# Weights requested one matrix at a time, behind a tile's value steps: attention and a mixture of experts in one kernel

## The chip, the cores and the metric

The kernel runs on one core of a Trainium2 chip. A core has a tensor engine for matmuls (PE, with its weight loads shown as PEld), a vector engine (DVE), a scalar engine (ACT), GpSimd (POOL) and a sync engine (SP). The five run their own instruction streams and meet through semaphores. In this kernel SP and POOL issue nearly all DMA transfers. The metric is the device time of one execution in microseconds (us); lower is better.

## The reference

Two stages follow each other. The first is attention of 16 query heads over one shared key and value head, for 8 batches of 384 positions and a head size of 64. Its output is laid out as 3072 tokens of 1024 numbers. The second stage sends each token to one of 16 experts, chosen in two steps (one of 4 groups, then one of 4 experts of the group), and scales the expert's output by the product of the two softmax weights:

```python
scores = scale * np.matmul(q, k.transpose(0, 1, 3, 2))
attn = np.exp(scores - np.max(scores, axis=-1, keepdims=True))
attn = attn / (np.sum(attn, axis=-1, keepdims=True) + 1e-09)
x = (attn @ v).transpose(0, 2, 1, 3).reshape(B * S, H * D)      # 3072 x 1024
...
g_idx = np.argmax(x @ w_group, axis=1)                           # one of 4 groups
e_idx = np.argmax(xg @ w_expert[g], axis=1)                      # one of its 4 experts
h = np.maximum(xg[mask_e] @ w1[g, e], 0.0)
out[tok_idx] = (g_w * e_w)[:, None] * (h @ w2[g, e])
```

## The kernel before

**Tiles and slots.** A batch is 3 tiles of 128 positions, and a tile is 4 slots of two units; a unit is the scores of two heads for one tile. So there are 24 tiles (`NT`) and 96 slots (`NSL`), 12 to a batch (`SB`). `s0 = 12 * b` is the first slot of batch b, and `p = i % 4` is the place of slot i in its tile. One Python loop over the slots writes out the order of all instructions; nothing reorders them later.

**One slot**, in order: the scores of two units on PE (L161); the maximum on DVE (L169) and the exponential on ACT (L172); then the slot's middle. In slots 0 and 1 of a tile the middle holds queries being transposed on PE (L147) and pieces of an expert's work (`advance`). In slots 2 and 3 it holds half each of the values of the tile before (`pv`, L209: 96 matmul records per half, small ones, 32 rows deep). Then come the transposes of probabilities by DVE (L193), the normalization by POOL (`norm`, L187), and, after slot 3, `pv_out`: ACT copies the values to `xt` (L222) and POOL casts them to bf16 into `xb` (L223). Last in the slot stands what was put down for it under the key `"g"`, which is mostly DMA issues.

**What is put down for which slot.** `at(slot, where, fn, ...)` makes the entry and `run(slot, where)` carries it out. For batch b, the router's logits of its first tile come from slot `s0 + 8` on (L230, L247). The 128 tokens of that tile elect the batch's main expert: `gate_pick` at `s0 + 10` leaves its number in `idx`. `load_main(b, 0)` reads the number into a register of POOL and issues the expert's first matrix; `load_main(b, 1)` issues the second. A matrix is two DMAs on POOL's queue (`load_w`, L394), each 2 MB of fp32 in memory that becomes 1 MB of bf16 in SBUF. SP's queue takes in the same part of the batch the saved `xb` (`keep_xb`, L410), the keys and values of the next batch (L111, L112, L120) and queries (L105), in the order written, and the stores of the expert's output `y` (L476), each as soon as ACT has scaled it.

**Experts.** `main_expert(b)` begins at slot `12 * (b + 1) + 5`. It is a generator: it gives out 42 pieces, and `advance(n)` takes 3n of them, so that PE works on batch b's expert while it does the attention of batch b + 1. A group of three pieces is 8 matmuls and the eviction of their result: 8 groups with the first matrix (L419), then 6 groups with the second (L433). Each of the two matrices has two buffers.

**The end.** After the last slot come, written out by hand, the values of the last tile (`pv(NT - 1, 0, NB)`, both halves at once), the six groups left of batch 6's expert, the expert of batch 7, and a second expert for batch 7 (`second_expert`), whose number `gate_pick_second` finds at `s0 + 13`. Its two matrices are issued by `load_second(0)` and `load_second(1)`. Then a loop runs over (batch, expert) pairs that are not covered by then. In the profile below it has no turn to make.

Of the kernel before, what the change touches and what calls it, by code (L numbers as in the profile page):

```python
# [19 lines left out]
def kernel(  # L20
# [12 lines left out]
    B, H, S, D = q.shape  # L33
# [7 lines left out]
    FO = F // P  # L41
# [149 lines left out]
    def transp(u):  # L191

        nc.vector.transpose(  # L193
            out=ring[:, (u // 4) % 3, u % 4].rearrange("p h s -> p (h s)"),
            in_=st.pop(("pr", u))[:].rearrange("p h s -> p (h s)"),
        )

    def pv(t, n0, n1):

        v_sb = st["v", t // ST]  # L200
        a, z = sorted(((2 * t) % 3, (2 * t + 1) % 3))
        if n0 == 0:
            st["o", t] = [xbank() for _ in range(P // 32)]
        o = st["o", t]
        for n in range(n0, n1):
            for i in range(P // 32):
                r = slice(32 * i, 32 * (i + 1))
                for h in range(2):
                    nc.tensor.matmul(  # L209
                        out=o[i][h * D:(h + 1) * D, 0:2 * P].rearrange("d (g c q) -> d g c q", g=2, c=4),  # L210
                        lhsT=v_sb[r, n, :], rhs=ring[r, a:z + 1:z - a, :, h, ts(n, 32)],
                        start=(n == 0), stop=(n == NB - 1), tile_position=(32 * i, h * D),
                    )

    def pv_out(t):
        b, j = t // ST, t % ST
        xt = pool.tile([P, KO, P], FP32, tag="xt", name="xt", bufs=1)
        st["xt", b, j] = xt
        if j == 0:
            st["xb", b] = pool.tile([P, KO, S], BF16, tag="xb", name="xb", bufs=2)  # L220
        for i, o in enumerate(st.pop(("o", t))):
            nc.scalar.copy(out=xt[:, :, ts(i, 32)], in_=o[:, 0:2 * P].rearrange("p (c q) -> p c q", c=KO))  # L222
        nc.gpsimd.tensor_copy(out=st["xb", b][:, :, ts(j, P)], in_=xt[:])  # L223
# [167 lines left out]
    def load_w(e, n):  # L391
        w = wpool.tile([P, KO, F], BF16, tag=f"w{n + 1}", name="w")
        for o in range(0, KO, 4):
            nc.gpsimd.dma_start(  # L394
                out=w[:, o:o + 4, :], in_=(w1f, w2f)[n][ds(e, 1), :, o:o + 4, :].rearrange("o p c f -> (o p) c f")
            )
        return w

    def load_main(b, n):
        if n == 0:  # L400
            st["e", b] = nc.gpsimd.value_load(st.pop(("idx", b))[0:1, 0:1], min_val=0, max_val=GE - 1)
        st.setdefault(("w", b), []).append(load_w(st["e", b], n))

    def load_second(n):
        if n == 0:
            st["e2"] = nc.gpsimd.value_load(st.pop("idx2")[0:1, 0:1], min_val=0, max_val=GE - 1)
        st.setdefault("w_second", []).append(load_w(st["e2"], n))
# [4 lines left out]
    def expert(xb, w1, w2, result, psum, on_act=None):  # L412

        on_act = on_act or (lambda k: k % 2 == 0)
        h_t = pool.tile([P, FO, S], BF16, tag="hT", bufs=1)
        for fc in range(FO):
            hp = psum()
            for ko in range(KO):
                nc.tensor.matmul(  # L419
                    out=hp[:, 0:S], lhsT=w1[:, ko, ts(fc, P)], rhs=xb[:, ko, :], start=(ko == 0), stop=(ko == KO - 1)  # L420
                )
                if ko % (KO // 2) == KO // 2 - 1:
                    yield
            if on_act(fc):
                nc.scalar.activation(out=h_t[:, fc, :], in_=hp[:, 0:S], func=ACTF.Relu)  # L425
            else:
                nc.vector.tensor_scalar(out=h_t[:, fc, :], in0=hp[:, 0:S], scalar1=0.0, scalar2=None, op0=ALU.max)
            yield
        for j in range(ST):
            for nh in range(2):  # L430
                yp = psum()
                for fo in range(FO):
                    nc.tensor.matmul(  # L433
                        out=yp, lhsT=h_t[:, fo, ts(j, P)], rhs=w2[:, fo, ts(nh, 512)],
                        start=(fo == 0), stop=(fo == FO - 1),
                    )
                    if fo % (FO // 2) == FO // 2 - 1:
                        yield
                result(j, nh, yp, on_act(FO + 2 * j + nh))
                yield  # L440

    def scaled(gcol, store):

        ys = {}

        def result(j, nh, yp, by_act):
            if nh == 0:
                ys[j] = pool.tile([P, Dm], FP32, tag="y", name="y", bufs=3)
            y, g = ys[j], gcol()[:, j:j + 1]
            if by_act:  # L450
                nc.scalar.activation(out=y[:, ts(nh, 512)], in_=yp, func=ACTF.Copy, scale=g)
            else:
                nc.vector.tensor_scalar(out=y[:, ts(nh, 512)], in0=yp, scalar1=g, scalar2=None, op0=ALU.mult)
            if nh == 1:
                store(j, y)

        return result
# [13 lines left out]
    def main_expert(b, on_act):  # L471
        w1, w2 = st.pop(("w", b))

        def store(j, y):
            if b < B - 1:
                nc.sync.dma_start(out=out_v[b, :, j, :], in_=y[:])  # L476
            else:
                st["y", j] = y

        yield from expert(st["xb", b], w1, w2, scaled(lambda: st["gsel", b][0], store), any_bank, on_act)  # L480
# [22 lines left out]
    pending = []  # L503

    def advance(groups):
        for _ in range(3 * groups):
            while pending:
                try:
                    next(pending[0])
                    break  # L510
                except StopIteration:
                    pending.pop(0)
# [3 lines left out]
    def at(slot, where, fn, *args):  # L516
        later.setdefault((slot, where), []).append((fn, args))

    def run(slot, where):
        for fn, args in later.pop((slot, where), []):  # L520
            fn(*args)
# [4 lines left out]
    for b in range(B):  # L526
        s0 = SB * b
        for j in range(ST):
            x = s0 + 4 * j + 8
            at(x, "m2", logits, b, j)  # L530
            at(x, "w", logits_out, b, j)
            at(x + 1, "m0", logits2, b, j)
            at(x + 1, "v", logits2_out, b, j)
        for x, j0, j1 in ((s0 + 9, 0, 1), (s0 + 17, 1, ST)):
            at(x, "v", lambda b=b, j0=j0, j1=j1: st.__setitem__(("gm", b), gate_masks(b, j0, j1)))
            at(x, "v", lambda b=b: [next(st["gm", b]) for _ in range(3)])
        if b == 0:
            at(s0 + 10, "s", gate_choose, b)
            at(s0 + 10, "b", gate_score, b)
        else:  # L540
            at(s0 + 9, "m2", gate_choose, b)
            at(s0 + 9, "w", gate_score, b)
        at(s0 + 10, "w", gate_pick, b)
        at(s0 + 10, "g", load_main, b, 0)
        at(s0 + (11 if b == B - 1 else 10), "g", load_main, b, 1)
        at(s0 + 16, "g", keep_xb, b)
        at(s0 + 20, "m0", gate_count, b)
        at(s0 + 20, "v", gate_counted, b)
        x = s0 + (20 if b == B - 2 else 23)
        at(x, "w", lambda b=b: st.__setitem__(("gv", b), gate_values(b)))  # L550
        at(x, "w", lambda b=b: [next(st["gv", b]) for _ in range(3)])
        if b == B - 1:
            at(s0 + 13, "w", gate_pick_second, b)
            at(s0 + 13, "g", load_second, 0)
        if b + 1 < B:
            at(s0 + 4, "g", load_k, b + 1)
            at(s0 + 4, "g", load_v, b + 1)
            at(s0 + 8, "m0", prep_batch, b + 1)
            at(s0 + 8, "v", prep_out, b + 1)
# [72 lines left out]
    b = B - 1  # L632
    i = NSL
# [5 lines left out]
    run(i, "w")  # L639
    transp(2 * i - 2)  # L640
    transp(2 * i - 1)
    advance(1)
    run(i + 1, "m0")
    run(i + 1, "v")
    run(i + 1, "w")
    run(i + 1, "g")
    pv(NT - 1, 0, NB)
    pv_out(NT - 1)
    advance(2)
    run(i + 4, "m2")  # L650
    run(i + 4, "w")
    run(i + 4, "g")
    advance(1)
    run(i + 5, "m0")
    run(i + 5, "v")
    pending.append(main_expert(b, lambda k: k < FO or k % 2 == 0))
    advance(1)
    load_second(1)
    pending.append(second_expert(None))
    advance(2)  # L660
    run(i + 8, "m0")
    run(i + 8, "v")

# [95 lines left out]
```

## Time and profile before

| | |
|---|---|
| median of 3 runs | 558.66 us (555.86 to 561.7) |
| the profiled execution | 560.02 us, span 558.6 us |
| mean granted clock of PE | 0.991 |
| busy share | PE 95%, DVE 75%, ACT 61%, POOL 48% |
| chain that ended last | PE 88%, DVE 6%, ACT 3%, issue 2% |
| weights (L394) | 36 DMAs, 1024 KB each, median 18.7 us from issue to landing |
| POOL's time to issue one of them | 777 ns |
| moved on POOL's queue / SP's and ACT's data | 37.75 MB / 36.04 MB |
| memory traffic | 92.88 MB read, 18.87 MB written, 200 GB/s over the span |

Three things help to read the profile. "Busy" is the time in which an engine has an instruction at work; for PE the ends of matmuls are modelled. An idle stretch is put down to its releaser, the event that ended it, and "issue" means that nothing in the profile released it. DMA queues have numbers: q0 is POOL's queue, which carries the weights, q1 is SP's and ACT's data, and q8 and q14 carry instructions.

The batches repeat. In the profiled execution the expert's first matmuls of one batch and the next begin 62 to 63 us apart. At the end, the last scores are followed by these stretches on PE: values of the last tile from 491.7 to 502.4 us, the last expert's first matrix from 509.5 us, its second from 520.3 us, the second expert's matrices from 530.6 and 541.0 us, and the last matmul ends at 551.5 us.

### The profile page before, as it was taken

To read this page: it belongs to the slowest core of one execution; us is meant where nothing else is said; L and a number is where in the kernel's file an instruction comes from. 1 tells how busy PE (TensorE), PEld (TensorE's weight loads), DVE (VectorE), ACT (ScalarE), POOL (GpSimd) and SP (SyncE) were. 2 spreads that over 40 slices of the span, in tenths; PEclk is the share of its full clock that TensorE was granted. 3 is DMA by queue.
4 is the path that set the end of the run, shared out by engine and by line. 5 is a ranking of instruction groups with operands and counts; after the bars stand their busy time and mean duration, and the time that the engine had idled before them with its cause. 6 is when DMAs were issued, how large, how long until landed. Compare 5 with 4: busy or idle time off the path is not lost.

```text
span 558.6 us, 17530 instructions
## 1 busy us (share of the span) xinstructions
PE 530.6 (95%) x7074; PEld 310.1 (56%) x7074; DVE 418.4 (75%) x847; ACT 339.2 (61%) x1043; POOL 270.6 (48%) x456
## 2 busy tenths in 40 slices
PE   7598899999999999999999999999999999979994
PEld 3255456655665556655665556655665555555452
DVE  4989988877888778877888678876888778823322
ACT  4776666666666666766666676676666676613210
POOL 2655954564457444565447535555447535622000
PEclk9999999999999999999999999999999999989999
DMA  7710993099805993099706992199706960299923
GB/s 118 161 30 13 177 229 75 2 195 233 202 2 97 210 250 77 4 200 247 181 1 111 213 262 48 11 211 247 164 2 111 213 189 2 29 212 263 222 51 115
DMA packets 98098, 75.15 MB, mean 135 GB/s; under 512 B 75104, under 2 KB 75104, under 8 KB 98016
## 3 DMA queue, kind: packets, MB, share of 16 engines
q0 software_dynamic: 19008, 37.75, 38.1%
q1 hardware_dynamic: 78080, 36.04, 24.7%
q8 instruction: 57, 0.93, 0.7%
q10 hardware_dynamic: 928, 0.23, 0.2%
q14 instruction: 25, 0.20, 0.1%
HBM read 92.88 MB, written 18.87 MB: 200 GB/s over the span
## 4 chain that ended last, share of the span: by engine, by line
PE 88%; DVE 6%; ACT 3%; issue 2%; ACTq 0%; DVEq 0%
PE x L209 24%; PE s L161 22%; PE x L419 13%; PE x L433 11%; PE sb L433 6%; PE sb L419 4%; PE x L147 3%; DVE nmx L169 3%; ACT pr L172 3%; PE x L230 2%; DVE ring L193 2%; PE x L247 1%; PE x L94 1%; PE x L129 0%; PE x L338 0%
## 5 line engine op out<-in xcount | busy, mean ns | idle before, releaser
L187 POOL TENSOR_SCALAR pr<-pr,rinv 128x384 f32<-128x384 f32 x384 | 218.2, 591 | 222.6 <-DVE rinv L183 222.6
L172 ACT ACTIVATE pr<-s,nmx 128x384 f32<-128x384 f32 x384 | 217.9, 580 | 139.6 <-DVE nmx L169 133.1
L169 DVE TENSOR_REDUCE nmx<-s 128x2 f32<-128x768 f32 x192 | 174.4, 948 | 58.0 <-PE s L161 57.8
L193 DVE STREAM_TRANSPOSE ring<-pr 128x768 f32<-128x768 f32 x192 | 175.4, 952 | 0.0
L161 PE MATMUL s<-kt,qt 64*128 64x384 f32 x768 | 152.8, 511 | 13.0 <-ACT pr L172 12.8
L209 PE MATMUL x<-ring,v_sb 32*64 32x256 f32 x4608 | 142.5, 382 | 5.8 <-issue 4.8
L209 PEld LDWEIGHTS x<-ring,v_sb 32*64 32x64 f32 x4608 | 103.5, 132 | 47.8 <-issue 28.9
L161 PEld LDWEIGHTS s<-kt,qt 64*128 64x128 f32 x768 | 65.1, 186 | 71.5 <-ACT pr L172 37.3
L419 PE MATMUL x<-xb,w 128*128 128x384 bf16 x448 | 79.5, 326 | 0.0
L172 ACT ACTIVATION_READ_ACCUMULATOR pr<-s,nmx 128x1 f32 x384 | 77.9, 203 | 0.0
L419 PEld LDWEIGHTS <-w 128*128 128x128 bf16 x576 | 56.6, 100 | 32.0
L433 PEld LDWEIGHTS <-h_t 128*128 128x128 bf16 x432 | 41.3, 100 | 50.4 <-issue 9.1
L433 PE MATMUL x<-w,h_t 128*128 128x512 bf16 x288 | 68.2, 379 | 0.0
L222 ACT COPY xt<-x 128x256 f32<-128x256 f32 x96 | 29.1, 391 | 13.5 <-PE x L209 13.1
L425 ACT ACTIVATE h_t<-x 128x384 bf16<-128x384 f32 x56 | 28.2, 506 | 9.4 <-PE x L419 8.8
L433 PE MATMUL sb<-w,h_t 128*128 128x512 bf16 x144 | 33.2, 388 | 0.0
L394 POOL DMA_DIRECT2D w<-in_moe_w_dram x36 | 27.5, 777 | 10.5 <-PE x L247 5.6
L151 ACT COPY qt<-x 128x512 f32<-128x512 f32 (+1 forms) x49 | 29.0, 594 | 2.7 <-PE x L147 2.7
L239 DVE COPY lt<-x 128x128 f32<-128x128 f32 x24 | 6.7, 278 | 31.7 <-PE x L230 31.6
L147 PE MATMUL x<-ident,q_sb 128*128 128x128 f32 x192 | 29.5, 277 | 0.0
L147 PEld LDWEIGHTS x<-ident,q_sb 128*128 128x128 f32 x192 | 23.7, 143 | 8.9 <-issue 1.6
L223 POOL CAST xb<-xt 128x1024 bf16<-128x1024 f32 x24 | 24.9, 1040 | 7.5 <-ACT xt L222 7.5
(83 smaller groups left out, 217.5 us busy)
## 6 DMA issues: line engine op xcount, KB each, us to landing
w<-in_moe_w_dram POOLq DMA_DIRECT2D x36, 1024.0 KB, 18.7
q_sb<-in_q_dram SPq DMA_DIRECT2D x23, 512.0 KB, 6.4
out_dram<-y SPq DMA_DIRECT2D x21, 512.0 KB, 8.3
xb_scratch<-xb SPq DMA_DIRECT2D x8, 768.0 KB, 5.5
v_sb<-in_v_dram SPq DMA_DIRECT2D x32, 96.0 KB, 4.2
out_dram<-y SPq DMA_DIRECT2D x6, 256.0 KB, 2.0
kk<-in_k_dram SPq DMA_DIRECT2D x15, 96.0 KB, 5.4
q_sb<-in_q_dram SPq DMA_DIRECT2D x1, 256.0 KB, 4.1
```

The source lines that it names most:

```text
L147: nc.tensor.transpose(out=pt[:, ts(c, P)], in_=q_sb[:, h:h + 2, :].rearrange("p t d -> p (t d)"), identity=ident[:])
L151: nc.scalar.copy(out=qt[:, r], in_=pt[:, r])
L161: nc.tensor.matmul(out=s[:, h, 0:S], lhsT=qt[r, ts(cc, P)], rhs=kt[r, :], start=True, stop=True)
L169: nc.vector.tensor_reduce(out=nmx[:], in_=s[:, :, 0:S], axis=AX.X, op=ALU.max, negate=True)
L172: nc.scalar.activation(out=pr[:, h, :], in_=s[:, h, 0:S], func=ACTF.Exp, bias=nmx[:, h:h + 1], scale=1.0, accum_out=ssum[:, k, h:h + 1],)
L187: nc.gpsimd.tensor_scalar(out=pr, in0=pr, scalar1=rinv[:, k, h:h + 1], scalar2=1.0, op0=ALU.mult, op1=ALU.mult)
L193: nc.vector.transpose(out=ring[:, (u // 4) % 3, u % 4].rearrange("p h s -> p (h s)"), in_=st.pop(("pr", u))[:].rearrange("p h s -> p (h s)"),)
L209: nc.tensor.matmul(out=o[i][h * D:(h + 1) * D, 0:2 * P].rearrange("d (g c q) -> d g c q", g=2, c=4), lhsT=v_sb[r, n, :], rhs=ring[r, a:z + ...
L222: nc.scalar.copy(out=xt[:, :, ts(i, 32)], in_=o[:, 0:2 * P].rearrange("p (c q) -> p c q", c=KO))
L419: nc.tensor.matmul(out=hp[:, 0:S], lhsT=w1[:, ko, ts(fc, P)], rhs=xb[:, ko, :], start=(ko == 0), stop=(ko == KO - 1))
L425: nc.scalar.activation(out=h_t[:, fc, :], in_=hp[:, 0:S], func=ACTF.Relu)
L433: nc.tensor.matmul(out=yp, lhsT=h_t[:, fo, ts(j, P)], rhs=w2[:, fo, ts(nh, 512)], start=(fo == 0), stop=(fo == FO - 1),)
```

## The change

For batches 0 to 6 the two matrices were both issued at the end of slot `s0 + 10`, which is slot 2 of a tile. Now the first is issued at the end of `s0 + 11` (slot 3, behind that tile's `pv_out`) and the second at the end of `s0 + 15` (slot 3 of the next tile). For batch 7 the first matrix stays at `s0 + 10`. Its second matrix, before at `s0 + 11`, and the second expert's first matrix, before at `s0 + 13` and ahead of the last values, are now issued behind the last `pv_out`. Two of the six groups left of batch 6's expert move from behind the last values to ahead of them. The last expert's first group comes one group earlier relative to the router's small matmuls (L247).

```diff
         at(s0 + 10, "w", gate_pick, b)
-        at(s0 + 10, "g", load_main, b, 0)
-        at(s0 + (11 if b == B - 1 else 10), "g", load_main, b, 1)
+
+        at(s0 + (10 if b == B - 1 else 11), "g", load_main, b, 0)
+        if b < B - 1:
+            at(s0 + 15, "g", load_main, b, 1)
...
             at(s0 + 13, "w", gate_pick_second, b)
-            at(s0 + 13, "g", load_second, 0)
...
     transp(2 * i - 2)
     transp(2 * i - 1)
-    advance(1)
+    advance(2)
     run(i + 1, "m0")
     run(i + 1, "v")
     run(i + 1, "w")
-    run(i + 1, "g")
+    advance(1)
     pv(NT - 1, 0, NB)
     pv_out(NT - 1)
+    load_main(b, 1)
+    load_second(0)
     advance(2)
     run(i + 4, "m2")
     run(i + 4, "w")
     run(i + 4, "g")
+    pending.append(main_expert(b, lambda k: k < FO or k % 2 == 0))
     advance(1)
     run(i + 5, "m0")
     run(i + 5, "v")
-    pending.append(main_expert(b, lambda k: k < FO or k % 2 == 0))
     advance(1)
     load_second(1)
     pending.append(second_expert(None))
-    advance(2)
+    advance(1)
     run(i + 8, "m0")
     run(i + 8, "v")
```

## The prediction

> **What bounds the kernel now.** I read the page first, then the waits of the tensor engine (PE), then its timeline, and last the DMA views cut into short windows.
>
> ```profile
> PE 530.6 (95%) x7074; PEld 310.1 (56%) x7074; DVE 418.4 (75%) x847; ACT 339.2 (61%) x1043; POOL 270.6 (48%) x456
> ...
> PE   7598899999999999999999999999999999979994
> ...
> PEclk9999999999999999999999999999999999989999
> DMA  7710993099805993099706992199706960299923
> ...
> q8 instruction: 57, 0.93, 0.7%
> ```
>
> PE is 95% busy, and from slice 6 on it hardly rests: a batch takes what PE's own work takes. Work saved on POOL, which issues the weights, is worth nothing by itself. What can move the time is idle PE. The DMA row swings between idle and full once a batch; the full slices are the weights.
>
> ```profile
> PE s L161 <- ACT pr L172: 12.8, 23, 1.6
> PE x L209 <- issue: 4.8, 5, 2.9
> ```
>
> The first wait is the start (11.9 of the 12.8 us lie before 70 us, with no expert to fill in). The second is in the value matmuls (L209) and has no engine behind it. Their timeline shows it:
>
> ```profile
> 190.91 1.95 PE L209 MATMUL x<-ring,v_sb 32*64 32x256 f32 x54
> 193.36 1.53 PE L209 MATMUL x<-ring,v_sb 32*64 32x256 f32 x42 [0.50 <-issue]
> ...
> 498.75 3.69 PE L209 MATMUL x<-ring,v_sb 32*64 32x256 f32 x57 [2.92 <-issue]
> 502.38 4.73 PE L433 MATMUL sb<-w,h_t 128*128 128x512 bf16 x16
> ```
>
> An undisturbed half tile of values (96 records) takes 2.85 us. The second half tile behind each weight request takes longer: by 1.0, 0.6, 1.1, 0.05, 1.0, 1.0 and about 0.1 us in batches 0 to 6, some 5 us in all.
>
> I take this for **late instructions**. Queue q8 carries 57 packets of 16 KB (0.93 MB); PE has 14148 matmul and weight-load records, so a packet is some 250 of them. Counting PE's records in order, each one, the gaps of batches 0, 2, 4, 5 and the last tile come after records 1472, 5056, 8640, 10432 and 13760: all 192 above a multiple of 256. Narrow DMA windows put an instruction packet 1.3 to 1.6 us before each gap's end (packet of 0.9 us at 191.0, values resume at 193.4; 496.3 and 498.75). Counted from the boundary before, that packet starts within 0 to 1.5 us when no weights run, after 2.9 to 3.7 us (mean 3.3) under weights in six of the value pairs, and after 4.5 us at 496.3, where 4 KB store packets run too. A block must last until the next is there: 3.3 + 0.9 + 1.4 = 5.6 us under load. Two half tiles of values and the scores between use a block in 4.9 us, hence a stall of some 0.7 us; elsewhere a block lasts 6 to 15 us, and nothing shows.
>
> ```profile
> 490.00:495.00 5.00, 4.72 (x130) 4.05 (x135) 2.64 (x9) 0.69 (x1) 1.74 (x4) 1.00 1.05 177
> 495.00:500.00 5.00, 2.08 (x49) 1.43 (x40) 0.00 (x0) 0.00 (x0) 0.67 (x1) 0.78 1.10 249
> 500.00:505.00 5.00, 5.00 (x49) 2.31 (x33) 0.00 (x0) 1.29 (x4) 1.04 (x1) 0.54 1.12 212
> ```
>
> In these windows (busy time of PE, PEld, DVE, ACT, POOL, then clock, DMA share, GB/s) the last tile's stall also halves the granted clock, to 0.54. From 485.3 to the last expert's start at 509.5 PE needs six groups of L433 (1.73 us each), 5.55 us of values and 1.5 us of small matmuls: 17.4 us of 24.2. So 6.8 us are lost there.
>
> **The change, part by part.** Same instructions, other order.
>
> *First matrix of batches 0 to 6, one slot later* (behind a value pair). Its two DMAs leave POOL behind the cast L223 instead of behind the slot before, about 6.3 us later (110.4 to 116.7 in batch 1). The next value pair starts at 124.3.
>
> ```profile
> DMA to landing us min/median/max: 8.6/12.0/15.5
> ```
>
> That row is one matrix (the two DMAs at 484.6 and 485.4): the second lands 16.3 us after the first is issued. So matrix 1 is in flight from 118 to about 131 and still covers the next pair; its boundary at 124.8 has 5 to 6 us of load ahead, and in the other batches at least 4, more than the 3.3 us. The old queue depth is no help in the rows: with the last one or two DMAs left the packets start as late as with four. **Gain: 0** of the 5 us; bounds 0 and 5.0, where a shorter queue would free the fetch. It is used at 139.8 (L419, batch 1), 8 us after landing: no wait.
>
> *Second matrix, slot 15* (behind the following pair). It leaves POOL behind this cast, at 135.0 in batch 1:
>
> ```profile
> 134.00 1.04 POOL L223 CAST xb<-xt 128x1024 bf16<-128x1024 f32 x1
> ```
>
> Behind it on POOL is the normalization at 138.7; the two issues cost 1.5 us and are over by 136.6: 0. It is in flight until about 151, and the next value pair is at 145.7 to 152.8, which was free of weights. **This is the new cost.** Blocks that begin at such a pair and last 4.9 us come at 270.3, 333.1, 396.3 and 458.7 (batches 3 to 6); in batches 0 to 2 they last 6.0 to 7.9 us. The casts there end at 260.2, 322.0, 384.7 and 447.6, so the boundaries come 10 to 12 us after the request, inside the load. Price each: at the 3.3 us of the earlier pairs 0.7 us; at the 4.5 us of 496.3, 4.5 + 0.9 + 1.4 - 4.9 = 1.9 us. Here the store of y and of xb (4 and 6 KB packets) run in the same stretch, as at 496.3; I take the middle, 1.2 us: **+4.8 us**, bounds 0 and 8.4 (with 0.8 for batch 2, at 6.0 us).
>
> SP's transfers move from an empty DMA into this load. How they share:
>
> ```profile
> q0 software_dynamic: 715, 1.43, 94.3%
> q1 hardware_dynamic: 713, 0.18, 17.3%
> ```
>
> This is 127 to 135 us: packet for packet, so 256-byte packets get through at 90 per us against 900 without weights (2737 in 3 us at 147). The keys kk are 768 such packets behind 256 of y and xb. In batch 1 I get weights until 151.4, kk landing near 153.7, and their transposes (L129) at 154.5; in batches 0 and 3 the two are within half a us, in the others kk is 1.5 to 2 us ahead. **+0.5 us**, bounds 0 and 5. Queries are behind kk, land near 158 and are read at 161.6: 0. The query load at 118.4, which took 20.9 us, gets faster, but nobody waited for it (read at 141.1).
>
> *The end.* The first matrix stays at 484.6. Two groups of L433 move ahead of the last values, so these start at 494.9. The boundary is now 32 records ahead of them (491.7), the block lasts until 498.1, and its successor, at 4.5 us, is usable at 498.5: the stall shrinks to about 0.4 us, no halved clock. Values end at 500.8, xt at 502.1, the cast at 503.2: the last expert starts **6.3 us earlier**, its first half (10.9 us) ends at 514.1.
>
> But its second matrix is now asked for at 503.2 instead of 489.35. With y and xb (256 large packets) beside it I count its 1024 packets of 2 KB from 504.7 on: 128 beside y until 507.3, 127 beside xb until 510.7, 769 at the 106 per us of 520 to 525 us until 518.0, and 1.4 for the slow first packets and the landing: 519.4. (The row's 16.3 us gives 519.5.) Four L433 matmuls go on the first half, then PE waits 4 us, and behind that L433 stands all that is left: the second expert and the last stores. The row for what such a wait does is the 2.92 us one: clock halved until about 504.6, 3 us lost. The start's waits of up to 1.6 us did not halve it. I take 2 us: second half over at 519.4 + 9.6 + 2.0 = 531.0, against 530.8 before. The second expert's matrices follow at 9.7 us each (529, 539), needed at 531.0 and 541.5: hidden. **+0.2 us**; bounds -1.8 (clock kept; then its first matrix is the limit) and +4 (a landing 2 us later and the full 3 us).
>
> Sum: +4.8 + 0.5 + 0.2 = 5.5. The profiled execution was 560.02 us (span 558.6), 1.4 above the median of 558.66. So 565.5 as profiled, 564 as a median.
>
> One rule speaks against this. The Trainium skill (Runtime: NRT & Kernel Launch, Instruction fetch mechanics) has instructions come in blocks of 256, prefetched ahead, with the boundary mostly hidden. The trace agrees on the block and not on the hiding, as the gaps at the 192nd record show. By that rule the +4.8 would fall away, and the sum would be 559.4.
>
> **The rivals.**
> 1. *A matrix alone does not hold up the fetch* (not slower). Two short loads leave the instruction queue room; the stalls of matrix 1 shrink, matrix 2 adds none. For it: batch 3 lost only 0.05 us, so 0.4 us less delay is enough for most. Against: packets were as late with one or two DMAs left. All 5.0 us gained, tail -1.8 to +0.2: 552 to 554; half of it 556. It decides from a fetch start of 2.6 us (4.9 - 0.9 - 1.4).
> 2. *Nothing new in the steady part*: the second matrix is done, or the packet early enough, at those four boundaries. Old stalls stay, the tail cancels: 558.5 to 560. (For it: in batches 0 to 2 that is what I expect anyway. Against: 4.9 us is less than the 5.6 us counted.) The skill's rule above ends here.
> 3. *The last expert waits longer than it gained*: second matrix at 521.5 and the clock halved through two windows as at 497.8 to 504.6, second half over near 534.5 (+3.7), with 1.9 us at each of the four boundaries (+7.6): 558.7 + 11.3 = 570. For it: that clock row. Against: the matrix alone in the ring.
>
> **How the numbers follow.** The forecast, with 0.45, spans 560.5 to 567.5. Rival 1 has 0.20, rival 2 0.20, rival 3 0.15. A measurement of this kernel can tell about 1% from no change (553.1 to 564.2). Slower by over 1%: 0.30 of the forecast's 0.45 and all of rival 3: 0.45. Faster by over 1%: the better part of rival 1, 0.15. The rest 0.40. The range of 553 to 569 takes in all but the ends of rivals 1 and 3.
>
> **What would show it.** Right: L209 gaps with "issue" still behind matrix 1 and new ones near 275, 338, 401 and 463; none over 1 us in the last tile; a wait of L433 of some 4 us near 515, with the clock row below 9 there. Wrong: no gaps at those boundaries, or L433 going on at 514 without a wait, which would mean a matrix lands in under 12 us.

## The result, and the profile after

The changed kernel takes 564.84 us (median of 6 runs, 564.24 to 567.25). The kernel before, run beside it, takes 557.64 us (median of 6, 555.86 to 561.7). The ratio is 1.013, with a 95% interval of 1.0091 to 1.0169. The forecast was 564.0 us. The profiled execution of the changed kernel took 564.9 us (span 563.5), that of before 560.02 (span 558.6): the two profiles are 4.9 us apart and the medians 7.2, because the profiled execution of before was 2.4 us longer than its median. What follows accounts for the 4.9 us; where the profiled execution of before was long is said under "The end" below.

The page of the changed kernel, rows 1 and 2:

```profile
PE 529.6 (94%) x7051; PEld 309.5 (55%) x7074; DVE 417.4 (74%) x847; ACT 339.0 (60%) x1043; POOL 269.7 (48%) x456
...
PE   7598899999999999999999999999999999997795
...
PEclk9999999999999999999999999999999999999798
DMA  7710779069932999079932998089922991389953
```

PE does the same work (its weight loads are all there; 23 matmul records are missing from this trace). Its one loose slice near the end (the 36th before, 489 to 503 us) is full now, and the two that follow, 507 to 535 us, are not. The granted clock dips in the 38th slice (521 to 535 us) and no longer in the 36th. The DMA row has two bumps per batch, one per matrix, where it had one wide one.

PE's waits in the changed kernel (us in total, times, longest):

```profile
PE s L161 <- ACT pr L172: 13.0, 23, 1.6
PE sb L433 <- DMA w<-in_moe_w_dram: 6.6, 2, 3.9
PE x L129 <- DMA kk<-in_k_dram: 2.4, 3, 1.0
...
PE x L209 <- issue: 1.1, 2, 0.7
```

The wait of L209 for nothing visible went from 4.8 to 1.1 us. This row leaves out the shorter stops: what went is the 2.9 us of the last tile, while the half tiles of the batches lost 5.0 us in all before and lose 5.1 now. Two new rows stand above it: the last expert's L433 waits for its second matrix, and the transposes of the keys (L129) wait for their DMA. PE's timeline shows where. First the batches:

```profile
154.59 0.52 PE L129 MATMUL x<-ident,kk 128*128 128x128 f32 x3 [1.03 <-DMA kk<-in_k_dram]
217.74 0.52 PE L129 MATMUL x<-ident,kk 128*128 128x128 f32 x3 [0.81 <-DMA kk<-in_k_dram]
...
317.10 2.39 PE L209 MATMUL x<-ring,v_sb 32*64 32x256 f32 x75
320.20 1.08 PE L209 MATMUL x<-ring,v_sb 32*64 32x256 f32 x21 [0.71 <-issue]
...
401.88 3.58 PE L209 MATMUL x<-ring,v_sb 32*64 32x256 f32 x96
464.72 3.42 PE L209 MATMUL x<-ring,v_sb 32*64 32x256 f32 x96
```

The keys' transposes wait in three batches (two are shown). The pair at 317 us is the one behind the first matrix, with its pause. The half tiles at 401.88 and 464.72 lie behind the second matrix and take 3.4 to 3.6 us instead of 2.85. Then the end:

```profile
497.48 5.43 PE L209 MATMUL x<-ring,v_sb 32*64 32x256 f32 x192
505.33 1.46 PE L419 MATMUL sb<-xb,w 128*128 128x384 bf16 x8
519.07 1.04 PE L433 MATMUL sb<-w,h_t 128*128 128x512 bf16 x3 [2.66 <-DMA w<-in_moe_w_dram]
524.05 11.85 PE L433 MATMUL sb<-w,h_t 128*128 128x512 bf16 x44 [3.95 <-DMA w<-in_moe_w_dram]
```

The last tile's 192 value matmuls run through without a pause, and the last expert starts sooner behind them. But its second half then waits twice, once for each DMA of its matrix. The windows from 515 to 530 us (busy time of PE, PEld, DVE, ACT, POOL, then clock, DMA share, GB/s) show what the second wait brings:

```profile
515.00:520.00 5.00, 2.29 (x12) 1.03 (x12) 1.74 (x10) 0.98 (x2) 0.00 (x0) 1.00 1.11 217
520.00:525.00 5.00, 1.05 (x4) 0.39 (x3) 0.00 (x0) 0.00 (x0) 0.00 (x0) 0.67 1.12 211
525.00:530.00 5.00, 5.00 (x17) 1.86 (x16) 0.75 (x1) 0.69 (x1) 0.00 (x0) 0.65 1.13 213
```

The clock falls to 0.67 and 0.65, and the group of 44 matmuls takes 11.85 us; where no long wait stood ahead of it, the same group took 9.66 (shown below).

### The profile page after: what moved, and what is told of

The parts are those of the page before. It is cut to its first block, busy times and chain, and to the rows that moved or that the text cites. A ratio compares the mean times of both kernels' runs of the same rounds, so it can differ in the third digit from the quotient of the medians.

```text
span 563.5 us, 17505 instructions
## 1 busy us (share of the span) xinstructions
PE 529.6 (94%) x7051; PEld 309.5 (55%) x7074; DVE 417.4 (74%) x847; ACT 339.0 (60%) x1043; POOL 269.7 (48%) x456
## 4 chain that ended last, share of the span: by engine, by line
PE 73%; DMA 11%; DVE 6%; issue 4%; ACT 3%; POOL 1%; SPq 1%; POOLq 0%; ACTq 0%; DVEq 0%
PE s L161 19%; PE x L209 19%; PE x L433 11%; PE x L419 11%; DMA kk<-in_k_dram 8%; PE sb L433 4%; DMA w<-in_moe_w_dram 3%; DVE nmx L169 3%; PE x L147 3%; ACT pr L172 3%; PE sb L419 2%; DVE ring L193 2%; PE x L230 2%; PE x L247 1%; PE x L94 1%
## 5 line engine op out<-in xcount | busy, mean ns | idle before, releaser
L209 PE MATMUL x<-ring,v_sb 32*64 32x256 f32 x4608 | 140.9, 379 | 1.9 <-issue 1.1
L209 PEld LDWEIGHTS x<-ring,v_sb 32*64 32x64 f32 x4608 | 102.7, 131 | 43.8 <-issue 25.6
L433 PEld LDWEIGHTS <-h_t 128*128 128x128 bf16 x432 | 41.6, 100 | 57.7 <-issue 14.3
L433 PE MATMUL x<-w,h_t 128*128 128x512 bf16 x270 | 67.2, 379 | 0.9
L433 PE MATMUL sb<-w,h_t 128*128 128x512 bf16 x139 | 34.2, 398 | 6.9 <-DMA w<-in_moe_w_dram 6.6
## 6 DMA issues: line engine op xcount, KB each, us to landing
kk<-in_k_dram SPq DMA_DIRECT2D x15, 96.0 KB, 14.7
```

The source lines that it names most:

```text
L209: nc.tensor.matmul(out=o[i][h * D:(h + 1) * D, 0:2 * P].rearrange("d (g c q) -> d g c q", g=2, c=4), lhsT=v_sb[r, n, :], rhs=ring[r, a:z + ...
L433: nc.tensor.matmul(out=yp, lhsT=h_t[:, fo, ts(j, P)], rhs=w2[:, fo, ts(nh, 512)], start=(fo == 0), stop=(fo == FO - 1),)
```

## The experiments

The theory going in: the stalls in L209 are late blocks of PE instructions, so the change costs time where a second matrix now runs beside a value pair, and at the end through the late second matrix of the last expert. The rivals: the batches cost nothing and all comes from the end, or the other way round; or the gaps have nothing to do with instruction blocks. Gaps are given as what a half tile of values takes beyond 2.85 us, added up over the batches; the half tile near 47 us, which is long in every run, is left out. All ratios are to the kernel before, run on the same chip in the same session (558.56 us for the first four, 557.32 for the next four, 557.58 for the last).

**The batches alone.** The new requests of batches 0 to 6; the end as before.

```diff
-        at(s0 + 10, "g", load_main, b, 0)
-        at(s0 + (11 if b == B - 1 else 10), "g", load_main, b, 1)
+        at(s0 + (10 if b == B - 1 else 11), "g", load_main, b, 0)
+        at(s0 + (11 if b == B - 1 else 15), "g", load_main, b, 1)
```

> The batches' part of the change alone: the first matrix of batches 0 to 6 behind slot s0+11, the second behind s0+15; the end as before. My theory: the batches lose a little, because the second matrix now runs beside the next batch's keys and the following value pair. In the trace of after the last slots' work ends 2.65 us later than before (first L433 of the end at 487.9 against 485.3), so this kernel should be 2 to 4 us slower than before (about 560), with PE waits at L129 for the keys in batches 1 to 3 and value gaps near 275, 339, 402 and 465. Rival: the loss of after sits in the end alone; then this kernel is at 557.6, within 1 us.

561.91 us; ratio 1.0069 (1.0048 to 1.0089), 3.9 us by the ratio. New gaps came at 274, 401 and 464 us (2.0 us together), none near 339. The waits for the keys that were expected did not come: 0.3 us in all in this profiled execution, with the keys landing at most 0.5 us ahead of PE's first matmul on them. Counted over all of PE's records, its semaphore waits and other control records included (matmuls and weight loads alone give no fixed place), every pause of over 0.3 us in the values of the batches and the first one in the last tile come 193 or 194 records above a multiple of 256 (the prediction has 192), the new ones too. The last tile stalls as before:

```profile
500.08 2.88 PE L209 MATMUL x<-ring,v_sb 32*64 32x256 f32 x57 [2.75 <-issue]
```

**The end alone.** Batches as before; the end as in the changed kernel.

> The end's part of the change alone: batches as before, end as in after (two groups ahead of the last values, the last expert's second matrix and the second expert's first behind them). My theory: the stall of the last values and the halved clock behind it go (6 us gained), and the wait for the second matrix with its own halved clock takes it all back and 2.5 us more, as the two traces stand (end 68.7 us against 66.3): 2 to 3 us slower than before, about 560, PE waiting at L433 some 6.6 us in two pieces. Rival: the end is worth nothing (the two cancel) and all of the loss is in the batches: 557.6, within 1 us.

560.96 us; ratio 1.0048 (1.0030 to 1.0067), 2.7 us. Its timeline shows the same long wait and the same slow group:

```profile
521.81 11.95 PE L433 MATMUL sb<-w,h_t 128*128 128x512 bf16 x44 [3.96 <-DMA w<-in_moe_w_dram]
```

Both halves of the change cost something, and 0.69% and 0.48% add up to 1.2%, within the interval of the whole (1.3%). Neither rival that blames one half alone holds.

**The end's groups alone.** Only the order of the expert's groups from the new end; every weight request stays where it was, also the second expert's first matrix ahead of the last values.

```diff
-    advance(1)
+    advance(2)
...
     run(i + 1, "g")
+    advance(1)
     pv(NT - 1, 0, NB)
...
+    pending.append(main_expert(b, lambda k: k < FO or k % 2 == 0))
     advance(1)
...
-    pending.append(main_expert(b, lambda k: k < FO or k % 2 == 0))
     advance(1)
     load_second(1)
     pending.append(second_expert(None))
-    advance(2)
+    advance(1)
```

> Only the order of the expert's groups at the end is that of after: two groups more ahead of the last values. Every weight request stays where it was before. My theory: the stall in the last values came from a block of instructions that began with them and had to last only 3.7 us; with 32 records more ahead of them the block lasts 6.4 us, so the stall falls from 3.3 us to 0.5 or none, the clock stays, nothing waits for weights: 5 to 6.5 us faster than before, about 552. Rival: the weights in flight slow or stall the values wherever they stand; then the gap stays at about 3 us and the time at 557.6.

554.04 us; ratio 0.9923 (0.9898 to 0.9948), 4.3 us faster, a little less than expected. Timeline, and the window in which the values run:

```profile
494.07 5.44 PE L209 MATMUL x<-ring,v_sb 32*64 32x256 f32 x192
...
515.10 9.66 PE L433 MATMUL sb<-w,h_t 128*128 128x512 bf16 x44 [1.24 <-DMA w<-in_moe_w_dram]
```

```profile
495.00:500.00 5.00, 5.00 (x171) 3.89 (x156) 0.00 (x0) 0.44 (x2) 1.48 (x2) 1.00 1.08 281
```

The weights run at full rate (DMA share 1.08) beside the values, and there is no stall: the 32 records put ahead of the values are enough. What is lacking against the expectation is about the size of a new wait of 1.24 us for the second matrix, behind which the clock stays at 1.00.

**The last expert's second matrix early.** The new end, but with that one matrix asked for at `s0 + 11` as before; the second expert's first matrix stays behind the last values.

Against the changed kernel:

```diff
-
-        at(s0 + (10 if b == B - 1 else 11), "g", load_main, b, 0)
-        if b < B - 1:
-            at(s0 + 15, "g", load_main, b, 1)
+        at(s0 + 10, "g", load_main, b, 0)
+        at(s0 + (11 if b == B - 1 else 10), "g", load_main, b, 1)
...
     pv_out(NT - 1)
-    load_main(b, 1)
     load_second(0)
```

> As e2 (end of after, batches as before), but the last expert's second matrix is asked for where it was before, at s0+11; the second expert's first matrix stays behind the last values. My theory: the wait at L433 is the price of asking for that matrix at 503 instead of 489; it is gone here, the stall of the values stays away (the block lasts 6.4 us and the packet comes after 4.5 us at the worst), and the second expert's first matrix lands near 520 against 524 needed: 5 to 6.5 us faster than before, about 552, like the kernel with only the groups moved. Rival: what counts is whether weights run beside the last values; then the values stall again by 3 us with the halved clock, and the time is 557 to 559.

554.42 us; ratio 0.9919 (0.9896 to 0.9943). That is the time of the groups alone, and like it somewhat less than the 5 to 6.5 us expected. So asking late for the second expert's first matrix costs nothing, and the late second matrix of the last expert is the whole price of the new end: 560.96 - 554.42 = 6.5 us.

**The first matrix back by one slot.** As the batches alone, but with the first matrix at `s0 + 10` again.

```diff
-        at(s0 + (10 if b == B - 1 else 11), "g", load_main, b, 0)
+        at(s0 + 10, "g", load_main, b, 0)
```

> As e1 (second matrix behind s0+15, end as before), but the first matrix of batches 0 to 6 is asked for at s0+10 again, now alone. My theory: a matrix is in flight some 13 to 15 us; asked for at s0+10 it is over when the next value pair begins (about 125 against a block boundary at 124.8 in batch 1), so the old stalls behind it go or shrink to under 0.3 us each, 3 to 4.5 us less than e1: 556 to 558.5. The new cost of the second matrix (keys at L129, value gaps of batches 3 to 6) stays. Rival: the stalls belong to the second half of the old request or to the slot, not to what is in flight at the pair; then the time is that of e1, 560 to 562.

560.05 us; ratio 1.0041 (1.0015 to 1.0068), some 1.6 us less than the batches alone and not the 3.4 or more expected; the two intervals overlap, so the time alone decides nothing. The trace does: the gaps behind the first matrix are gone in batches 1 to 6 (1.0 us left, in batch 0, against 4.1). Batch 4, where before and after the change a half tile lost over 1 us:

```profile
313.77 2.85 PE L209 MATMUL x<-ring,v_sb 32*64 32x256 f32 x96
...
318.04 2.85 PE L209 MATMUL x<-ring,v_sb 32*64 32x256 f32 x96
```

In the DMA trace the first matrix's packets end at 315.2 us here, 0.1 us after the block boundary, and the instruction packet starts 1.2 us behind that boundary instead of 3.3. But the gaps behind the second matrix stay (2.3 us in all), and the keys now wait more:

```profile
PE x L129 <- DMA kk<-in_k_dram: 3.4, 4, 1.3
```

**Three requests.** The second matrix in two single DMAs, at `s0 + 15` and `s0 + 19`; the first at `s0 + 10`; the end as before. Against the kernel before (`load_second_half` issues one DMA of the matrix and is left out here):

```diff
-        at(s0 + (11 if b == B - 1 else 10), "g", load_main, b, 1)
+        if b == B - 1:
+            at(s0 + 11, "g", load_main, b, 1)
+        else:
+            at(s0 + 15, "g", load_second_half, b, 0)
+            at(s0 + 19, "g", load_second_half, b, 4)
```

> First matrix at s0+10, the second in two requests of one DMA each, behind s0+15 and behind s0+19; end as before. My theory: one DMA is in flight 6 to 8 us and fits between two value pairs (14 us apart), and the first matrix is over before the next pair; so no block that begins in a value pair meets weights, the steady gaps at L209 and the waits for keys are gone, and only the last tile's stall is left: 4 to 5.5 us faster than before, about 553 (ratio 0.991). Rival: the value gaps have another cause than weights in flight at a pair; then 557 to 560.

555.66 us; ratio 0.9965 (0.9944 to 0.9986), 1.9 us faster, where more was expected. Nothing waits for the keys any more. Of the batches' gaps 2.9 us are left, among them one of 1.2 us in batch 5:

```profile
399.76 1.94 PE L209 MATMUL x<-ring,v_sb 32*64 32x256 f32 x51 [0.55 <-issue]
```

Its packet started 3.0 us behind a boundary at which the weights had just ended (393.9 and 393.5 us). The DMA engines were not empty: 6 KB packets of xb ran until 395.2 us, and behind them 256-byte packets of SP's loads. The kernel before has the same boundary at 396.3 us, beside such loads and no weights, and its packet came after 2.2 us. But in batch 0 of the three requests a packet came 2.8 us behind its boundary (69.4 us) although no other packet had started since 69.6 us. So weights are not the only thing that makes a packet late; what else does stays open.

**Records moved, no DMA.** The kernel before, with its 7 warm-up matmuls at the start replaced by 85 short ones. No transfer and no later instruction changes its place; only the count of PE records ahead of everything grows by 156.

```diff
-    def busy(n):
+    def busy(n, cols=512):
...
-            nc.tensor.matmul(out=x[:], lhsT=blank[:, 0:P], rhs=blank[:], start=True, stop=True)
+            nc.tensor.matmul(out=x[:, 0:cols], lhsT=blank[:, 0:P], rhs=blank[:, 0:cols], start=True, stop=True)
...
-    busy(7)
+    busy(85, 32)
```

> Before, with the 7 warm-up matmuls of 512 columns replaced by 85 of 32 columns: all of PE's stream stands 156 records later, and no DMA is moved. My theory (late instruction blocks of 256 records): a gap needs a block boundary in the first 144 records of a value pair that meets weights. With the shift that holds in batches 0 and 1 alone, so the gaps of batches 2, 4 and 5 are gone and those of 0 and 1 stay; in the last tile the boundary moves into the 384 records of values, and the stall stays near 3 us but comes after about 177 of the 192 matmuls instead of 135. Time 2 to 3.5 us below before, if the start does not get longer. Rival: weights slow PE's reads of values whatever its instructions are; then the gaps stay in batches 0, 1, 2, 4 and 5 and the last one after about 135 matmuls.

554.47 us; ratio 0.9944 (0.9924 to 0.9965), 3.1 us faster. In batch 4 the gap is gone although both matrices are in flight as before, and in the last tile the pause has moved from the records around 135 to the 185th of 192 (and, at 1.63 us, is shorter than the 3 us expected):

```profile
316.52 2.85 PE L209 MATMUL x<-ring,v_sb 32*64 32x256 f32 x96
...
490.77 5.41 PE L209 MATMUL x<-ring,v_sb 32*64 32x256 f32 x185 [0.28 <-DVE lg L251]
497.81 0.66 PE L209 MATMUL x<-ring,v_sb 32*64 32x256 f32 x7 [1.63 <-issue]
```

The pause follows the count of instructions, not the data: here too all four pauses over 0.3 us come 193 or 194 records above a multiple of 256. Gaps of 0.7 to 1.0 us stayed in batches 0 and 1, as expected. This shows the mechanism on which the forecast rests. By the rule of the Trainium skill that was weighed against it (Runtime: NRT & Kernel Launch, Instruction fetch mechanics: the boundary is mostly hidden) this edit would have moved nothing. Under weights the boundary is not hidden: PE stood for 1.63 us in the last line above. The measurement decides.

**Three requests and the groups.** The last two gains together: the batches of the three requests, the end of the groups alone.

> The requests of e6 in the batches and the order of the groups of e3 at the end. My theory: the two gains have nothing to do with each other and add up, 4 to 5.5 us and 4.3 us: 547 to 549.5, ratio 0.982 to 0.985. Rival: they share a cause (the steady gaps come back elsewhere, or the end is set by the landing of the second expert's matrices); then no more than 5.5 us, 552 or above.

552.76 us; ratio 0.9911 (0.9875 to 0.9947). It has the lowest time of all and beats both kernels, yet falls short of the 547 to 549.5 us expected, which counted the first gain at 4 us or more. The two gains alone are 0.35% and 0.77%, 1.1% together, and 0.9% was measured, with an interval of 0.5% to 1.25%: whether they add up can't be told. Its ratio can't be told apart from that of the groups alone, measured on another chip. What it still waits for at the end is the second matrix:

```profile
PE sb L442 <- DMA w<-in_moe_w_dram: 1.3, 1, 1.3
```

**Keys earlier.** The changed kernel, with the keys asked for four slots sooner.

```diff
-            at(s0 + 4, "g", load_k, b + 1)
+            at(s0 + 4 if b == 0 else s0, "g", load_k, b + 1)
```

> The changed kernel, but with the next batch's keys asked for at the first step of a batch instead of four steps later (from the second batch on). Theory: the transposes of kk wait 2.4 us in the changed kernel because the keys queue behind the second matrix, and nothing is put in their place, so that these waits vanish and the time goes from 564.8 to 562 to 563 (ratio to before 1.008 to 1.010). Rival: the keys, asked for ahead, only push the second matrix and with it the instruction packets back, so that L129 waits no longer but the pauses in L209 behind the second matrix (1.8 us in the changed kernel) grow by as much: 564.5 to 565.5, ratio 1.012 to 1.015.

562.33 us (561.12 to 564.52); ratio 1.0091 (1.0070 to 1.0113), against 1.0130 for the changed kernel. The intervals of the two overlap, so the 2.2 us between them are likely rather than shown. The profile shows the wait itself gone; these are the transposes that stand at 154.59 and 217.74 above:

```profile
153.56 0.51 PE L129 MATMUL x<-ident,kk 128*128 128x128 f32 x3
215.96 0.51 PE L129 MATMUL x<-ident,kk 128*128 128x128 f32 x3
```

Against the 2.4 us saved, the gaps in L209 went from 5.1 to 6.0 us. Of this growth 0.8 us lie behind the first matrix and only 0.2 behind the second, where the rival put it. Behind the first matrix the batches alone, whose requests are those of the changed kernel, show as much (4.1 us against 3.4), so the rival's exchange is not shown.

## Why the prediction was right, and which of its terms were not

The time, its sign and the mechanism were right. That the sum came so close is partly luck: errors of both signs cancelled. By the medians, the batches alone cost 3.9 us (forecast 5.3) and the end alone 2.7 (forecast 0.2). In the two profiled executions, counting what each half tile of values takes beyond 2.85 us:

| term | predicted | measured | where |
|---|---|---|---|
| first matrix moved | 0 | -1.5 | gaps behind it 4.9 us before, 3.4 after |
| second matrix beside a value pair | +4.8 | +1.5 | 0.2 us before, 1.7 after |
| keys late | +0.5 | +2.4 | three waits of L129 |
| the end | +0.2 | +2.5 | from the first L433 of the end (485.27; 487.92) to the start of the last one: 65.9 us, now 68.4 |
| sum | +5.5 | +4.9 | the spans differ by 4.9 |

**First matrix: about right.** Gaps stayed behind it in most batches, as forecast; 1.5 us came back, inside the bounds of 0 and 5. Little of that is shown to be the change: with the requests of before, the other profiled executions had 3.6 to 4.2 us of these gaps (the end alone, its groups alone, the second matrix early), and with those of after 4.1 and 4.2 (the batches alone, keys earlier). Rival 1, that a matrix alone does not hold up the fetch, is refuted for this slot: in batches 1 to 6 packets started 2.5 to 3.6 us behind the boundary. One slot earlier they started after 1.0 to 2.2 us in batches 1 to 6, since the matrix was in by then, and the gaps were gone. So in these pairs what counts is whether weights still run just behind the boundary, not how many DMAs are queued.

**Second matrix: right places, mis-sized.** New gaps came at 275.0, 401.9 and 464.7 us, three of the four places named; the pair near 338 ran through. The term failed where it took the middle between the 3.3 us of the earlier pairs and the 4.5 us beside stores: the packets came after 2.6 to 3.0 us, no later than beside a lone matrix. With 2.9, the step's own formula (2.9 + 0.9 + 1.4 - 4.9) gives 0.3 us for each boundary, 1.2 us in all; 1.5 was measured. Three more executions with the second matrix at `s0 + 15` lost 1.9 to 2.3 us there.

**Keys: five times the forecast here, below it in another execution.** The second matrix stayed in flight at least 1.6 us longer than the 151.4 us counted for batch 1 (its last packets start at 153.0), and the 768 small packets of the keys came behind. Their median time to landing went from 5.4 to 14.7 us:

```profile
kk<-in_k_dram SPq DMA_DIRECT2D x15, 96.0 KB, 14.7
```

The bounds (0 and 5) held it. The keys land so close to their use that the sum is not steady: the batches alone, with the same requests and a median landing of 14.8 us, waited 0.3 us in all, the first matrix back 3.4. With the keys asked for earlier this wait vanished, and with the second matrix split it did too.

**The end: mis-sized within its bounds.** The last tile's stall went, as forecast, and the last expert started 17.4 us behind the first L433 of the end (forecast 17.9). The clock loss was 2.2 us (forecast 2). What failed was the landing of the second matrix. It left POOL at 505.2 us, 2.0 later than forecast, because the batches had lost 2.65 and the last expert started 0.5 sooner behind them. Moved by these 2.0 us, the forecast landing is 521.4; it came at 524.0. The DMA view of 507 to 511 and of 511 to 519 us shows it (packets, MB, share of 16 engines):

```profile
q0 software_dynamic: 148, 0.30, 64.0%
q1 hardware_dynamic: 86, 0.29, 29.4%
```

```profile
q0 software_dynamic: 613, 1.22, 81.9%
q1 hardware_dynamic: 143, 0.78, 25.2%
```

The forecast, moved, had the first weight packet at 506.7 us, the stores through at 512.7, and 106 weight packets per us from there. The first one started at 507.9, the 6 KB packets of xb ran until 517, and from 511 to 519 us only 77 per us went out beside them. So the 1024th weight packet started at 521.7, 1.7 us behind the moved forecast. The landing came another 2.3 us later, not 1.4: by then over 200 packets of the second expert's first matrix had started beside the last ones of this one. Its first half also came only at 519.0, and with it a wait of 2.66 us that the forecast did not have: it let four matmuls run on that half, from 514.1 on, without a wait.

The old end is not steady either. The last tile's pause was followed by a halved clock for 6.8 us in the profiled execution of before, and for 3.4 us in those of the batches alone, the first matrix back and three requests, where pauses were 2.4 to 2.8 us and the same stretch took 64.0 to 64.5 us instead of 65.9. That is most of the 2.4 us by which this execution exceeds its median, and against these three the new end costs about 4 us, where the medians say 2.7.

**What the forecast did not separate.** It booked the 6.3 us of an earlier start against the 4 + 2 us of the late matrix, as one step. They are two edits. The reordered groups need none of the moved requests: alone they are worth 4.3 us, and the late second matrix takes them back and 2.7 us more.

## What to carry to other kernels

When PE pauses with no releaser in the trace, count its records, control records included. Here pauses at a fixed place modulo 256, under DMA load, were late instruction blocks, and padding the stream or putting large, slow matmuls ahead of dense small ones moved or removed them without touching a transfer. Requests split into pieces must be judged by what still runs at each block boundary and by which small-packet loads now run beside them. And when a change bundles a reorder with a later request, price and try them apart: here one gained 4.3 us and the other lost 6.5 to 6.9.

## What the hardware showed that was not expected

- A late matrix does not cost its wait alone. After waits of 2.66 and 3.95 us the clock stood at 0.67 and 0.65 over 10 us, and 44 matmuls took 11.85 us instead of 9.66. A wait of 1.24 us ahead of the same 44 left them at 9.66. No limit in between is shown: in the start of the kernel with the second matrix early, a pause of 1.32 us was followed by 6.8 us at the halved clock.
- Seventy-eight more warm-up matmuls at the start made the kernel 3.1 us faster (ratio 0.9924 to 0.9965), and the gaps in the batches went from 5.0 to 2.4 us. Nothing else behind the start was changed but where the 256-record boundaries fall.
- An instruction packet under weights starts 2.5 to 3.7 us behind its boundary in the value pairs of batches 1 to 6, whether one matrix or two are queued. It started 1.0 to 2.2 us behind it where a lone first matrix ended within 1.3 us of the boundary, but 2.5 to 3.0 us behind it where half a second matrix had ended and 6 KB packets of xb ran on (three requests, batches 3 to 5).
